# Weight loads ahead of a waiting load on SyncE's queue, in a fused sparse-attention and mixture-of-experts kernel

## Chip, cores and metric

The kernel runs on one core of a Trainium2 chip. The metric is the device time of one execution in microseconds (us); lower is better. A profiled execution gives a trace. Its span runs from the first to the last instruction, and the execution's own time is a little longer than its span.

## What is computed

First a block-sparse softmax attention over 4 batches, 8 heads, 768 positions and 64 channels, all in float32. Each block of 32 queries sees its own and the two neighbouring key blocks, the first and the last block, and three blocks that an index table names; the first and the last query block see all keys. The result, reordered to 3072 tokens of 512 channels, goes into a soft mixture of 8 experts with 4 slots each:

```python
attn = softmax(where(mask, q @ k.T / 8, -1e9)) @ v
x = attn.transpose(0, 2, 1, 3).reshape(3072, 512)
logits = x @ phi                                   # 512 x 32
slot_input = softmax_over_tokens(logits).T @ x     # 32 slots
h = relu(slot_input[e] @ w1[e])                    # 512 -> 1024, per expert
slot_out[e] = h @ w2[e]                            # 1024 -> 512
out = softmax_over_slots(logits) @ slot_out
```

The slots need the softmax over all tokens, so the experts cannot start before the attention has ended. The expert weights w1 and w2 are 33.5 MB together, in 64 tiles of 128 partitions by 1024 floats (512 KB each).

## The kernel before

The attention is a list of 52 items: per batch 11 pairs of query blocks (`plan_pair`) and two dense halves (`plan_dense`) for the first and the last block. An item is a chain over the engines. GpSimd (POOL) and ScalarE (ACT) stage the key blocks (`kst`); TensorE (PE) makes the scores (`s`, L652; `sd`, L849); VectorE (DVE) takes row maxima (L669, L867); ACT takes exponentials (L674, L880); DVE turns them (`ptt`, L681; `ptd`, L884); PE multiplies with the values (`av`, `avd`, L746); DVE normalizes the result to `x` (L739 to L741). Transposes of `x` (`mxt`, L940), the logits (`ml`, L975) and the running slot sums (`ms`, L1025) follow per group of four query tiles. At the end of the attention four groups of logits are normalized (`cm`, `lst`, L1083 to L1100), split into two halves each (`c`, L1107 on DVE and L1113 on POOL) and transposed (`pc`, L1126) for the last matmul.

The order of this part is not the order of the source. A `Plan` object collects tasks with their dependencies and buffers; `plan` simulates the engines with fixed task costs and takes, among the tasks that can start soonest, the one with the smallest `turn`; `turn` is the task's key in items plus `BEHIND[kind]`, one number for each of 82 kinds of task. `run` then issues the tasks in that order inside a manual schedule, which keeps the issued order on PE, DVE, ACT and POOL, and inside a second one, which keeps it on SyncE (SP). All large DMAs are issued by SP, one after the other: an SP instruction that waits holds up all those behind it.

The planner also paces DMAs. It counts PE instructions in packets of 256 (a matmul of the program is four of them) and ties a paced DMA to a PE instruction at `MARK` = 56 instructions into a packet (`gate`); after `ROOM` = 0.55 MB behind one gate, or 1.4 us after it (`LATEST`), the next DMA has to take the next gate. `run` writes the tie as a wait on that PE instruction (`wait`).

The weights are loaded in the order in which the experts use them. Tiles 0 to 10 have places of their own (`wpre`) and come in during the attention. Tiles 11 to 25 go into places that the last batch leaves: the keys of the batch before (`ktile`, shown as `kw`), the values buffer `v0`, the buffer `ptd`, and then the keys' other buffer (`kw` again, tiles 23 to 25, the group with `n0 == 12`, from item 12 of the last batch on). These are tasks of the plan. The late tiles 26 to 43 are issued after `plan.run()` by `load_late`, one for each entry of `LORD`:

```python
LORD = [0, 1, 2, 3, 4, 5, -1, -2, -3, -4, 6, 7, 8, 9, -5, -6, 10, 11]
load_late(..., late + LATE * (2 * min(k, SLOW) + max(k - SLOW, 0)))
```

Entries from 0 on are places that the staging buffers of the attention leave (`lwb`, tile names w26 to w31, then w36 to w39) or places of `ptt`; negative entries are the six places in the values buffer `v1`, which the last matmuls of the attention read. Each of these loads waits on the last gate that the plan puts ahead of its due time. They are issued outside the second schedule, so on SP the framework's own scheduler decides their order. Tiles 44 to 63 take the places of tiles that the first expert layer has used (`done_w`, `next_w`).

The experts' two layers are `ffn1` (`pf`, L1370) and `ffn2` (`pso`, L1378), in two halves of the output columns. When the first half's slots are there, its outputs are made (`po`, L1474), copied (`ob`, L1476 and L1478) and stored between the experts of the second half; the second half's outputs follow at the end. At most eight SP DMAs are under way, since each waits for the landing of the one eight places before it.

Of the kernel before, what the change touches and what calls it, by code (L numbers as in the profile page):

```python
# [21 lines left out]
P = 128  # L22
# [20 lines left out]

LR, RATE = 64, 0.22
ROOM, AFTER, LATEST, NEXT = 0.55e6, 0.1, 1.4, 5.5
MARK, LATE, SLOW = 56, 1.1, 5

CS = 2
CW = DM // CS
# [1 line left out]
WP = 2048 // PW  # L51
# [11 lines left out]
E_ = mybir.EngineType  # L63
MAN = {E_.PE, E_.DVE, E_.Activation, E_.Pool}

BEHIND = {0: -25.15, 1: -115, 2: -27.9, 3: -173.9, 4: 29, 5: 50.5, 6: 234.65, 7: -47.25, 8: -98, 9: -36.5, 10: -8.25,
# [8 lines left out]
SOON = 0.03  # L75
LAG = {"DVE": 0.17, "ACT": 0.18, "POOL": 0.17, "SP": 0.0, "NONE": 0.0}
SP_COST = 0.55
# [32 lines left out]
class Plan:  # L110
# [30 lines left out]
    def plan(self, turn, best=1e9):  # L141
        T = self.tasks
        at = {e: 0.8 for e in ("PE", "DVE", "ACT", "POOL", "SP", "NONE")}
        mode, count, okay, room = "T", FIRST, 0.0, ROOM
# [13 lines left out]
        while avail:  # L158
            cand = []
            for t in avail:  # L160
                r, ok, k = ready[t], True, {}
                for p in need[t]:
                    i = (nxt[p] + k.get(p, 0)) % pools[p]
                    k[p] = k.get(p, 0) + 1
                    if held[p][i] or (p in queue and queue[p][qat[p]] != t):
                        ok = False
                        break
                    if slot[p][i] > r:
                        r = slot[p][i]
                if not ok:  # L170
                    continue
                if pace[t]:
                    r = max(r, at["SP"], gate + AFTER)
                    if r < gate + NEXT and (room <= 0 or r > gate + LATEST):
                        r = gate + NEXT
                st, en, e, d = 1e9, 1e9, None, None
                for o, c in opts[t]:
                    if o == "PE":
                        c = PE_TASKS[c]
                        s = at[o] if c[2] == mode else at[o] + TURN[mode]  # L180
                        if r > s:
                            s = r
                        z = s + c[0]
                    else:
                        s = at[o] if at[o] > r else r
                        z = s + c
                    if s < st or (s == st and z < en):
                        st, en, e, d = s, z, o, c
                cand.append((st, turn[t], en, t, e, d))
# [5 lines left out]
            if pace[t]:  # L195
                if st >= gate + NEXT:
                    gate, room, gid = st, ROOM, None
# [108 lines left out]
def attn_moe_kernel(ctx, tc, qT, kT, vtab, sampled, phi, w1, w2, out):  # L306
# [847 lines left out]
    N = len(items)  # L1154
# [24 lines left out]

    m, n = NPRE, first[B - 1]  # L1180
    t_last = state.t_acc
    for tag, pool, n0, n1 in (("ktile", "k", 1, 3), ("v0", "v", 3, 6), ("ptd", "ptd", 5, 7), ("ktile", "k", 12, 13)):
        go = lambda j: [qks[min(N - 1, n + n0 + (n1 - n0) * j // KW[tag])]]
        a_w = add(lambda t, tag=tag: new_wk(tag), ("NONE", 0.0), go(0), N + m, acq=[(pool, [t_last])])
        for j in range(KW[tag]):
            parts = [(slice(r, r + LR), slice(0, WP)) for r in range(0, P, LR)]
            if n0 == 12:
                parts = [(slice(0, P), slice(0, WP))]
            for i, (r, c) in enumerate(parts):
                add(lambda t, m=m, tag=tag, j=j, r=r, c=c: load_wk(m, tag, j, r, c), ("SP", SP_COST), go(j) + [a_w],  # L1190
                    N + m + j + i / 4, byte=4 * WP * P // len(parts), pace=2 if n0 == 12 else 1)
        m += KW[tag]


# [92 lines left out]
    ms = tc.manual_schedule(engines=MAN)  # L1287
    ms.__enter__()
    plan.fill = max(qks.items())[1], lambda n: warm(None, n)
    with tc.manual_schedule(engines={E_.SP}):  # L1290
        plan.run()
    warm(None, 1)
    ssum = fin.tot
    att.close()
# [31 lines left out]
    def load_late(pool, j, due):  # L1326

        m = len(wpool)
        i = load_w(m, pool) if j is None else load_wk(m - j, pool.tag, j)
        plan.wait(i, [plan.names[k] for k, b in enumerate(plan.bounds) if b[2] + AFTER <= due][-1])  # L1330
        wpool.append(pool)
# [21 lines left out]
    for k, n in enumerate(LORD):  # L1353
        if n < 0:
            load_late(vw, -1 - n, late + LATE * (2 * min(k, SLOW) + max(k - SLOW, 0)))
        else:
            load_late(lw[n], None, late + LATE * (2 * min(k, SLOW) + max(k - SLOW, 0)))

    def done_w(n):

# [206 lines left out]
```

## Time and profile before

| | us |
|---|---|
| median of 3 runs (308.28, 311.31, 311.51) | 311.31 |
| the profiled execution's own time | 310.53 |
| its span | 308.8 |
| PE busy | 279.3 |
| DVE busy | 217.1 |
| POOL busy | 178.9 |
| ACT busy | 173.8 |

A row of the timeline gives the start, the length, the engine, line, operation and tiles and a count; in brackets stands the idle time before it and what ended it. `SPq` is SyncE's queue; a row of DMAs there is the time of issuing, not of the transfer. Attention and slot sums run to about 248.7 us, the experts from 248.75 us (the first `pf`) to 291.86 us (the last `pso`), the last outputs to 300.45 us (the last copy `ob`), and the stores to the end.

### The profile page before, as it was taken

Reading aid. Unit: us, or ns where it says so; the run is one execution under the profiler, and the core shown is the slowest. Engines: PE = TensorE matmul, PEld = TensorE weight load, DVE = VectorE, ACT = ScalarE, POOL = GpSimd, SP = SyncE. Lnnn points to the kernel's source line nnn. Section 1 sums busy time; section 2 is a strip of 40 time slices with the busy share of each in tenths; the row PEclk is TensorE's granted clock in tenths of the full one; section 3 lists DMA queues with packets and bytes.
Section 4 is the critical chain, followed back from the end, with each engine's and each line's share of the span. In section 5 each row is a group of like instructions: output and inputs, shape, how many; then the busy total and the mean of one; then the engine's idle time right before and its main releaser. Section 6 shows DMA issues by size and latency. Waiting matters only on the chain.

```text
span 308.8 us, 17460 instructions
## 1 busy us (share of the span) xinstructions
PE 279.3 (90%) x7177; PEld 195.4 (63%) x7177; DVE 217.1 (70%) x500; ACT 173.8 (56%) x525; POOL 178.9 (58%) x491
## 2 busy tenths in 40 slices
PE   8598999999999999999999999979998999988670
PEld 7168777567777686686776768658676734534260
DVE  7779978778899789989997699877794250112160
ACT  7965976754685876477777637747431411004250
POOL 6668699956559998745899757369654140000000
PEclk9979999999999999999999999999999999999976
DMA  7924555373254547345454666557644899999998
GB/s 242 242 52 129 145 142 132 98 190 90 89 143 139 145 133 192 88 108 138 136 142 130 172 160 155 150 140 188 171 140 143 290 413 409 408 408 407 393 330 288
DMA packets 27825, 60.27 MB, mean 195 GB/s; under 512 B 3553, under 2 KB 16994, under 8 KB 27746
## 3 DMA queue, kind: packets, MB, share of 16 engines
q1 hardware_dynamic: 27600, 59.03, 62.2%
q8 instruction: 56, 0.92, 1.3%
q14 instruction: 23, 0.19, 0.2%
q10 hardware_dynamic: 146, 0.13, 0.1%
HBM read 52.86 MB, written 6.29 MB: 192 GB/s over the span
## 4 chain that ended last, share of the span: by engine, by line
PE 65%; DMA 18%; DVE 7%; issue 3%; SPq 2%; ACT 1%; ACTq 0%
PE av L746 32%; DMA w<-in_w_dram 13%; PE s L652 13%; PE avd L746 7%; PE mxt L940 4%; DMA kw<-in_w_dram 3%; PE sd L849 3%; PE po L1474 2%; DMA ktile<-in_kT_dram 2%; PE ml L975 2%; PE ms L1025 2%; DVE ptt L681 2%; DVE x L741 1%; DVE nm L669 1%; SPq L333 1%
## 5 line engine op out<-in xcount | busy, mean ns | idle before, releaser
L593 POOL COPY vrs<-v 128x260 f32 x264 | 95.4, 405 | 27.7 <-PE av L746 17.2
L674 ACT ACTIVATE p<-s,nm 128x256 f32<-128x256 f32 x176 | 72.7, 475 | 13.5 <-DVE nm L669 11.5
L746 PE MATMUL av<-v,ptt 64*64 64x130 f32 (+2 forms) x1728 | 76.2, 288 | 0.5 <-issue 0.5
L746 PEld LDWEIGHTS av<-v,ptt 64*64 64x64 f32 (+2 forms) x1728 | 50.7, 133 | 25.6 <-issue 19.0
L681 DVE STREAM_TRANSPOSE ptt<-p 128x512 f32<-128x512 f32 x88 | 56.3, 682 | 3.8 <-ACT p L674 3.7
L669 DVE TENSOR_REDUCE nm<-s 128x2 f32<-128x512 f32 x88 | 55.2, 679 | 2.2 <-PE s L652 2.0
L652 PE MATMUL s<-kst,q 64*32 64x256 f32 x1408 | 51.1, 380 | 2.6 <-ACT pd L880 1.8
L746 PE MATMUL av<-vrs,ptt 64*32 64x130 f32 x2112 | 46.9, 278 | 2.7 <-issue 2.6
L575 ACT ACTIVATE kst<-ktile 128x128 f32 x186 | 41.4, 303 | 10.1 <-PE s L652 8.9
L569 POOL COPY kst<-ktile 128x384 f32<-128x384 f32 x88 | 42.4, 507 | 6.2 <-PE s L652 6.2
L652 PEld LDWEIGHTS s<-kst,q 64*32 64x32 f32 x1408 | 31.2, 106 | 13.0 <-POOL vrs L593 3.1
L746 PEld LDWEIGHTS av<-vrs,ptt 64*32 64x32 f32 x2112 | 36.4, 106 | 4.7 <-issue 4.3
L467 ACT COPY xT<-mxt 128x512 f32<-128x512 f32 (+1 forms) x22 | 12.4, 564 | 23.2 <-PE mxt L940 22.8
L746 PE MATMUL avd<-v,ptd 64*64 64x130 f32 x768 | 23.7, 271 | 1.8 <-DVE ptd L884 1.2
L746 PEld LDWEIGHTS avd<-v,ptd 64*64 64x64 f32 x768 | 21.9, 132 | 4.0 <-PE s L652 2.1
L613 POOL TENSOR_SCALAR q<-q 128x256 f32<-128x256 f32 x21 | 8.4, 404 | 22.2 <-DMA q<-in_qT_dram 22.2
L577 POOL COPY kst<-ktile 128x128 f32 x78 | 20.0, 295 | 0.0
L880 ACT ACTIVATE pd<-sd,nb 128x384 f32<-128x384 f32 x32 | 16.8, 577 | 5.4 <-DVE nb L875 4.7
L611 ACT ACTIVATE q<-q 128x256 f32<-128x256 f32 x27 | 11.1, 418 | 13.7 <-DMA q<-in_qT_dram 13.1
L739 DVE TENSOR_SCALAR rs<-av 128x8 f32<-128x8 f32 (+1 forms) x27 | 4.1, 153 | 20.3 <-PE av L746 20.2
L940 PEld LDWEIGHTS mxt<-ident,x 128*128 128x128 f32 x96 | 10.2, 141 | 12.6 <-PE sd L849 2.9
L940 PE MATMUL mxt<-ident,x 128*128 128x128 f32 x96 | 15.9, 286 | 2.4 <-DVE x L728 0.9
(122 smaller groups left out, 312.0 us busy)
## 6 DMA issues: line engine op xcount, KB each, us to landing
w<-in_w_dram SPq DMA_DIRECT2D x23, 512.0 KB, 10.2
v<-in_w_dram SPq DMA_DIRECT2D x12, 512.0 KB, 10.2
q<-in_qT_dram SPq DMA_DIRECT2D x47, 128.0 KB, 2.8
w<-in_w_dram SPq DMA_DIRECT2D x22, 256.0 KB, 4.1
out_dram<-ob SPq DMA_DIRECT2D x22, 256.0 KB, 3.9
ktile<-in_kT_dram SPq DMA_DIRECT2D x24, 192.0 KB, 3.4
v<-in_vtab_dram SPq DMA_DIRECT2D x16, 211.2 KB, 3.9
v<-in_vtab_dram SPq DMA_DIRECT2D x16, 195.0 KB, 3.5
```

The source lines that it names most:

```text
L467: ACT.copy(out=out, in_=in_)
L569: POOL.tensor_copy(out=st[:, :, w:w + 96], in_=kv[:, :, (i - 1) * BLK:(i + 2) * BLK])
L575: ACT.activation(out=st[:, :, o:o + BLK], in_=src, func=AF.Copy, scale=1.0)
L577: POOL.tensor_copy(out=st[:, :, o:o + BLK], in_=src)
L593: POOL.tensor_copy(out=st[:, :, j:j + 1, :], in_=vf[:, :, ds(t.vals[j], 1), :])
L652: PE.matmul(u.s[r][32 * p:32 * p + 32, j, :], lhsT=u.q[s_, p, j, :], rhs=kd[j][0][s_, p, :], start=True, stop=True)
L669: DVE.tensor_reduce(out=u.nm[r], in_=u.s[r], axis=AX.X, op=ALU.max, negate=True)
L674: ACT.activation(out=u.p[r][:, j, :], in_=u.s[r][:, j, :], func=AF.Exp, bias=u.nm[r][:, j:j + 1], scale=1.0)
L681: DVE.transpose(out=T.pt[r][:, :, 2 * w:2 * w + 2, :].rearrange("p k j q -> p j k q"), in_=u.p[r].rearrange("p j (k q) -> p j k q", k=8))
L746: PE.matmul(av[:, r * 2 * D1:(r + 1) * 2 * D1].rearrange("p (a d) -> p a d", a=2), lhsT=lhsT, rhs=rhs, start=start, stop=stop)
L880: ACT.activation(out=u.p[r][k], in_=u.s[r][k], func=AF.Exp, bias=u.nb[r], scale=1.0)
L940: PE.transpose(T.px[:, c, :], T.x[:, c * P:(c + 1) * P], ident)
```

## The change

Five edits; everything else is as before.

1. The schedule that keeps SP's issued order is left only after the loop over `LORD`, so the late loads stand in the order in which the source issues them.
2. The group of tiles 23 to 25 may start at item 11 of the last batch and not at item 12 (the `12` in its tuple and in the two comparisons is `11`).
3. A task of that group (`pace == 2`) is no longer sent to the next gate when the 0.55 MB are used up.
4. `LATE`, the step of the late loads' due times, is 1.0 us and not 1.1 us.
5. All 82 numbers of `BEHIND` are new.

```diff
-MARK, LATE, SLOW = 56, 1.1, 5
+MARK, LATE, SLOW = 56, 1.0, 5
...
-BEHIND = {0: -25.15, 1: -115, 2: -27.9, 3: -173.9, 4: 29, 5: 50.5, 6: 234.65, 7: -47.25, 8: -98, 9: -36.5, 10: -8.25,
+BEHIND = {0: 14.2, 1: -87.35, 2: 8.05, 3: -200, 4: -26.55, 5: 41.95, 6: 286.05, 7: -87.5, 8: 25.85, 9: -26.95, 10:
...
                 if pace[t]:
                     r = max(r, at["SP"], gate + AFTER)
-                    if r < gate + NEXT and (room <= 0 or r > gate + LATEST):
+                    if r < gate + NEXT and (room <= 0 and pace[t] == 1 or r > gate + LATEST):
                         r = gate + NEXT
...
-    for tag, pool, n0, n1 in (("ktile", "k", 1, 3), ("v0", "v", 3, 6), ("ptd", "ptd", 5, 7), ("ktile", "k", 12, 13)):
+    for tag, pool, n0, n1 in (("ktile", "k", 1, 3), ("v0", "v", 3, 6), ("ptd", "ptd", 5, 7), ("ktile", "k", 11, 12)):
...
-            if n0 == 12:
+            if n0 == 11:
                 parts = [(slice(0, P), slice(0, WP))]
...
-                    N + m + j + i / 4, byte=4 * WP * P // len(parts), pace=2 if n0 == 12 else 1)
+                    N + m + j + i / 4, byte=4 * WP * P // len(parts), pace=2 if n0 == 11 else 1)
...
-    with tc.manual_schedule(engines={E_.SP}):
-        plan.run()
+    ls = tc.manual_schedule(engines={E_.SP})
+    ls.__enter__()
+    plan.run()
...
             load_late(lw[n], None, late + LATE * (2 * min(k, SLOW) + max(k - SLOW, 0)))
+    ls.__exit__(None, None, None)
```

How this moves instructions. On SP, at the end of the attention, with the semaphores that each DMA waits for (`PE_49` is a wait on a PE instruction, `DMAHW` the wait for the DMA eight places before), the program had:

```order
L333 DMA ptd_67<-in_w1_dram 64x1024 [waits DMAHW3_49,PE_49]
L333 DMA kw_6562<-in_w1_dram 128x1024 [waits DMAHW4_49,PE_49,Activation_49]
L333 DMA kw_6562<-in_w1_dram 128x1024 [waits DMAHW5_49]
L333 DMA kw_6562<-in_w1_dram 128x1024 [waits DMAHW6_49,PE_49]
L333 DMA v1_69<-in_w2_dram 128x1024 [waits DMAHW7_49,PE_49,Pool_49]
L333 DMA w26_7026<-in_w1_dram 128x1024 [waits DMAHW0_49]
L333 DMA w27_7028<-in_w1_dram 128x1024 [waits DMAHW1_49]
L333 DMA w28_7030<-in_w1_dram 128x1024 [waits DMAHW2_49]
L333 DMA w29_7032<-in_w1_dram 128x1024 [waits DMAHW3_49]
L333 DMA w30_7034<-in_w1_dram 128x1024 [waits DMAHW4_49]
L333 DMA w31_7036<-in_w1_dram 128x1024 [waits DMAHW5_49]
```

and has now:

```order
L333 DMA ptd_67<-in_w1_dram 64x1024 [waits DMAHW3_49,PE_49]
L333 DMA kw_6517<-in_w1_dram 128x1024 [waits DMAHW4_49,Activation_49,Pool_49]
L333 DMA kw_6517<-in_w1_dram 128x1024 [waits DMAHW5_49]
L333 DMA kw_6517<-in_w1_dram 128x1024 [waits DMAHW6_49,PE_49]
L333 DMA w26_7025<-in_w1_dram 128x1024 [waits DMAHW7_49]
L333 DMA w27_7027<-in_w1_dram 128x1024 [waits DMAHW0_49]
L333 DMA w28_7029<-in_w1_dram 128x1024 [waits DMAHW1_49]
L333 DMA w29_7031<-in_w1_dram 128x1024 [waits DMAHW2_49,PE_49]
L333 DMA w30_7033<-in_w1_dram 128x1024 [waits DMAHW3_49]
L333 DMA w31_7035<-in_w1_dram 128x1024 [waits DMAHW4_49,PE_49,Pool_49]
L333 DMA v1_69<-in_w2_dram 128x1024 [waits DMAHW5_49,Pool_49]
```

The load into `v1` stood ahead of six loads and stands behind them. The values of the waits, counted in PE's matmuls of the program: before, the first `kw` waits for number 3211, the third for 3264 and the load into `v1` for 3342; now the third `kw` waits for 3211, w29 for 3277 and w31 for 3342. Number 3264 is the last matmul of the second last pair's `av`, 3277 the third and 3342 the 68th of the 84 of the last pair's. Behind these rows the two programs have the same loads in the same order.

On DVE the last item before was (`c` is the split of a group of logits, the `x` ahead of it is what PE's next transposes `mxt` read):

```order
L1100 TENSOR_TENSOR lst<-lst,cm 128x128
L681 STREAM_TRANSPOSE ptt<-p 128x2x8x32 x4
L739 TENSOR_SCALAR rs<-av 128x8
L740 RECIPROCAL rs<-rs 128x8
L741 TENSOR_TENSOR x<-av,rs 128x512
L1107 TENSOR_SCALAR c_6751<-lst 128x4x32 x2
```

and is now:

```order
L1100 TENSOR_TENSOR lst<-lst,cm 128x128
L681 STREAM_TRANSPOSE ptt<-p 128x2x8x32 x4
L1107 TENSOR_SCALAR c_6727<-lst 128x4x32 x2
L739 TENSOR_SCALAR rs<-av 128x8
L740 RECIPROCAL rs<-rs 128x8
L741 TENSOR_TENSOR x<-av,rs 128x512
```

One pair of `c` moved ahead of `x`. At the starts of the second, third and fourth batch DVE's order differs too, and in a like manner; at the last of them (the dense scores `sd`, with two transposes `ptt` of the pair before) it was:

```order
L681 STREAM_TRANSPOSE ptt<-p 128x2x8x32
L867 TENSOR_REDUCE nm<-sd 128x1 x2
L875 TENSOR_TENSOR nb_5207<-nm 128x1
L469 COPY d<-md 128x128
L867 TENSOR_REDUCE nm<-sd 128x1 x2
L875 TENSOR_TENSOR nb_5273<-nm 128x1
L884 STREAM_TRANSPOSE ptd<-pd 128x12x32 x2
L681 STREAM_TRANSPOSE ptt<-p 128x2x8x32
```

and is now:

```order
L681 STREAM_TRANSPOSE ptt<-p 128x2x8x32 x2
L469 COPY d<-md 128x128
L867 TENSOR_REDUCE nm<-sd 128x1 x2
L875 TENSOR_TENSOR nb_5266<-nm 128x1
L867 TENSOR_REDUCE nm<-sd 128x1 x2
L875 TENSOR_TENSOR nb_5274<-nm 128x1
L884 STREAM_TRANSPOSE ptd<-pd 128x12x32 x2
```

The second `ptt` and the copy `d` moved ahead of the maxima over `sd`. PE's own order differs in three places: twice a transpose `mxt` trades places with its neighbour `lt`, and once one moves a pair later. The DMAs ahead of the rows shown keep their order on SP and the PE instructions that they wait for.

16 rows, old and new, of the table BEHIND are left out of this document.

## The prediction

> **What bounds the kernel now.** I read the page's slices first, then the stretches of the last 90 us, then SyncE's queue, the chain, and PE's waits. The slices (40 of 7.72 us) show two different kernels:
>
> ```profile
> PE   8598999999999999999999999979998999988670
> DMA  7924555373254547345454666557644899999998
> GB/s 242 242 52 129 145 142 132 98 190 90 89 143 139 145 133 192 88 108 138 136 142 130 172 160 155 150 140 188 171 140 143 290 413 409 408 408 407 393 330 288
> ```
>
> Up to about 240 us PE is full and the DMA engines are half idle; from slice 32 on (247 us) the DMA engines are full at some 408 GB/s and PE has holes. So the last quarter is bound by how early the weight stream starts. The stretches around its start, with the columns PE, PEld, DVE, ACT, POOL, clock, DMA share and GB/s:
>
> ```profile
> 219.00:226.50 7.50, 7.46 (x224) 5.52 (x217) 5.30 (x16) 3.00 (x12) 4.50 (x13) 1.00 0.49 142
> 226.50:232.00 5.50, 4.85 (x111) 4.00 (x110) 5.33 (x17) 0.30 (x2) 2.79 (x8) 1.00 0.65 197
> 232.00:236.50 4.50, 4.50 (x163) 3.52 (x166) 1.55 (x4) 0.46 (x1) 2.70 (x7) 1.00 0.32 117
> 236.50:238.50 2.00, 1.14 (x26) 0.80 (x15) 1.48 (x10) 0.24 (x1) 0.00 (x0) 1.00 0.46 129
> 250.00:291.20 41.20, 36.06 (x418) 16.13 (x410) 8.08 (x24) 6.43 (x13) 3.57 (x6) 1.00 1.03 407
> 291.20:308.80 17.60, 7.46 (x38) 5.69 (x38) 5.52 (x11) 4.80 (x10) 0.00 (x0) 0.77 0.94 317
> ```
>
> Between 219 and 238.5 us the DMA engines move 117 to 197 GB/s; afterwards 407 until the last weight has landed, and in the last 17.6 us, stores of short rows, they are still 94% busy. Why the stream starts late is on SyncE's queue:
>
> ```profile
> 213.12 9.01 SPq L333 DMA_DIRECT2D ptd<-in_w_dram  x6
> 226.47 2.92 SPq L333 DMA_DIRECT2D kw<-in_w_dram  x3
> 236.48 0.33 SPq L333 DMA_DIRECT2D v<-in_w_dram  x1
> 236.86 5.16 SPq L333 DMA_DIRECT2D w<-in_w_dram  x6
> 242.06 5.89 SPq L333 DMA_DIRECT2D v<-in_w_dram  x3
> SPq L333 <- PE av L746: 28.6, 11, 7.0
> ```
>
> After the third `kw` (issued by 229.4 us) the queue stands still for 7.0 us, its longest wait, until the last `av` has read the values; the load into `v1` that waits stands ahead of six loads (w26 to w31) that wait for nothing. From there on the chain is the stream itself, each link being the landing that lets the DMA eight places later go:
>
> ```profile
> 240.11 9.79 DMA w<-in_w_dram
> 249.92 10.20 DMA w<-in_w_dram
> 260.18 10.16 DMA w<-in_w_dram
> 270.35 10.58 DMA kw<-in_w_dram
> 281.00 10.19 DMA w<-in_w_dram
> 291.22 0.64 PE pso L1378 x8
> ```
>
> Eight tiles take 10.2 us, so one tile of 512 KB costs 1.28 us, and the last expert matmuls start when the last tile lands.
>
> **The change, part by part.** *Late loads in the source's order (edit 1), with LATE (edit 4).* As the order of SyncE's queue shows, w26 to w28 now follow the third `kw` with no wait on an engine, w29 and w30 follow at matmul 3277 and w31 at 3342. Before, the first `kw` waited for 3211 and went at 226.47 us, and the `v1` load waited for 3342 and went at 236.48 us; these rows date the gates. Number 3277 is the third matmul of the last `av`, which starts at 231.8 us (row below). So the third `kw` goes at 226.5, w26 to w28 by about 228.5, w29 and w30 at about 232, w31 at 236.5 and the six `v1` loads behind it. Five tiles (w26 to w30) are moved ahead of 236.5 us, when the engines have room: the room from 226.5 to 236.5 us is ten us, and three `kw` and five tiles take 8 x 1.28 = 10.2 us. At 236.5 us the rest of the stream is five tiles shorter: 5 x 1.28 = **6.4 us**. The bounds of this term: at most 1.4 us more, if w30 is still under way when w31 goes, so that the start-up hole of 236.5 to 238.5 us (129 of 407 GB/s, 1.4 us lost) closes; at least 3 x 1.28 = 3.8 us, if w29 and w30 get no room ahead of w31.
>
> *The keys' old place one item sooner, and its pace (edits 2 and 3).* The first two `kw` lose their PE gate and follow the last `ptd`, which is issued by 222.1 us; the third, whose issue ended at 229.4 us, goes some 2 us sooner. What they wait for on ACT and POOL is staging of keys for the last scores, and these scores run at 221.6 us (first row below). That makes the room that the five tiles need (0.49 busy from 219 to 226.5 us); by itself it is worth nothing, since these tiles are used well after 250 us. Without it about two tiles less would fit: that is the lower bound just named.
>
> *Does the rest follow?* Behind w31 the queue's waits are on the eighth load before and on gates already passed, save w42, which waits for the matmul `msum`, and the loads from w44 on, which wait for the first expert layer:
>
> ```profile
> 221.57 1.12 PE L652 MATMUL s<-kst,q 64*32 64x256 f32 x31
> 247.24 0.36 PE L1224 MATMUL msum<-ssum,selw 128*128 128x1 f32 x2
> 248.75 4.92 PE L1370 MATMUL pf<-w,sT 128*32 128x512 f32 x42 [0.38 <-ACT sT L467]
> ```
>
> With 11 tiles (14 us) let go after 236.5 us the engines have work until after 250 us; `msum` runs at 247.2 us and the first layer starts at 248.75. It takes some 0.45 us for a tile (4.92 us for 11 tiles), so it frees places faster than the 1.28 us in which they are filled. No hole. On the other side PE must be able to finish sooner:
>
> ```profile
> 270.36 3.63 PE L1378 MATMUL pso<-w,hT 128*32 128x256 f32 x64
> 274.60 0.64 PE L1378 MATMUL pso<-w,hT 128*32 128x256 f32 x8
> 275.88 0.64 PE L1378 MATMUL pso<-w,hT 128*32 128x256 f32 x8 [0.64 <-DMA w<-in_w_dram]
> PE pso L1378 <- DMA w<-in_w_dram: 2.5, 4, 0.6
> PE pso L1378 <- DMA v<-in_w_dram: 1.6, 3, 0.6
> PE pso L1378 <- DMA kw<-in_w_dram: 1.1, 2, 0.6
> ```
>
> PE never waits for a tile before 274.6 us; after it, it waits 2.5 + 1.6 + 1.1 = 5.2 us up to 291.86 us. Taking just these out, the experts would end at 286.7. But eight such matmuls cost 0.64 us alone and 3.63 / 8 = 0.45 in a row, and 14 groups save another 2.6: 284.0 at best. With the stream 6.4 us ahead they end at 285.4, between the two: PE stops being idle just where the stream stops being late. So I keep 6.4, with 5.2 as a bound. The stores are behind the weights on the same saturated engines, so the end moves with the stream.
>
> *The new BEHIND table (edit 5).* DMAs ahead of `kw` keep order and gates, PE's order hardly changes, so it acts through DVE. The last item:
>
> ```profile
> 227.57 2.48 DVE L681 STREAM_TRANSPOSE ptt<-p 128x512 f32<-128x512 f32 x4
> 230.38 0.69 DVE L741 TENSOR_TENSOR x<-av,rs 128x512 f32<-128x512 f32 x1
> 230.98 2.56 DVE L1107 TENSOR_SCALAR c<-lst 128x128 int32<-128x128 int32 x8
> 231.21 0.63 PE L940 MATMUL mxt<-ident,x 128*128 128x128 f32 x4 [0.65 <-DVE c L1107]
> 231.84 4.58 PE av L746 x128
> ```
>
> PE already waits 0.65 us there, for `x`, with filler matmuls before it and the last `av` behind it. Two `c` now stand ahead of `x`: 2 x 2.56 / 8 = 0.64 us later, with nothing to hide it. **Loss 0.6 us**, and the gate 3342 is as much later. At the three batch starts one `ptt` (2.48 / 4 = 0.62) and one `d` copy (of the size of a `c`, 0.32) move ahead of the dense maxima, 0.9 us each. PE has the pair's `av` and the next scores to run meanwhile, so I cost it at nothing; without that cover it is 2.7 us lost, and a `ptt` that is ready sooner could give back as much.
>
> *PE's instructions.* They come by DMA too, and a load ahead of them can hold them up:
>
> ```profile
> q8 instruction: 56, 0.92, 1.3%
> 197.99 1.90 SPq L427 DMA_DIRECT2D q<-in_qT_dram  x2
> 199.94 1.11 SPq L333 DMA_DIRECT2D v<-in_w_dram  x2
> 204.15 0.43 PE L746 MATMUL av<-vrs,ptt 64*32 64x130 f32 x12 [1.63 <-issue]
> ```
>
> These are 56 packets of 16 KB, 256 instructions each. After 0.75 MB of loads PE stood 1.63 us with nothing else to wait for, the largest such hole. Now 2.1 MB (third `kw`, w26 to w28) go out just before the packet boundary near 232 us, and a packet lasts 128 matmuls there, 4.6 us. Of those 2.1 MB (4 x 1.28 = 5.1 us from about 228.5) some 1.6 us remain at 232, as much as 0.75 MB (1.8 us) did in the other place; but three `kw`, 1.5 MB, left no such hole. **Loss 0.3 us**, between 0 and 1.6.
>
> [...]
>
> The sum: 308.8 - 6.4 + 0.6 + 0.3 = **303.3 us** of span. The profiled execution took 310.53, 1.7 more than its span, so **305.0 us**. The median of the runs shown is 0.8 above that execution, their lowest 2.3 below; I make no correction.
>
> **The rivals.** *PE becomes the bound (B).* The experts end at 286.7 plus the 0.9 us lost before: gain 5.2 - 0.9 = 4.3, **306.2 us**. For it: the 0.64 us groups; against it: 0.45 us in a row. *Fewer tiles get ahead (C).* If only w26 to w28 find room, 3.8 - 0.9 = 2.9: **307.6 us**. For it: the gates of w29 and w31; against it: the share of 0.32 from 232 to 236.5 us. *The packet waits in line (D).* If PE's instructions wait behind all that is queued, six tiles (third `kw`, w26 to w30) are 7.7 us against the 4.6 that a packet lasts: a hole of 3.1 us, gain 6.4 - 0.6 - 3.1 = 2.7: **307.8 us**, hardly measurable. For it: the hole after 0.75 MB; against it: the three `kw` before. *DVE holds PE up (E), slower.* If at each of the three batch starts the dense scores wait for a full row of transposes, 2.48 us, the attention ends 3 x 2.48 + 0.6 = 8.1 us later, and every gate and the first layer with it: 308.8 + 8.1 - 6.4 = 310.5, that is **312.2 us**. It decides from 6.4 us of new stalls on. Against it: what moves is one transpose, not four, and PE's longest sum of waits for DVE before is at another place and small:
>
> ```profile
> PE avd L746 <- DVE ptd L884: 1.2, 2, 0.8
> ```
>
> **How the numbers follow.** Forecast (A) 0.57, B 0.18, C 0.08, D 0.11, E 0.06. The range: from 302.3 (6.4 + 1.4 without the small losses, and half a us of luck in the order) up to 308.8, past D and short of E, which leaves out some 0.15. A measurement here tells about 1% from no change, 3.1 us (the three runs lie 3.2 apart). Faster by more: all of A and B, half of C and a quarter of D, less a little for the scatter: 0.79. Within 1%: the rest of C and D and a part of E: 0.16. Slower: 0.05.
>
> **What would show it.** In SyncE's rows five `w` loads between 226 and 234 us and no wait of 7 us; over 300 GB/s from 228 to 236 us; the first `pf` at 249 to 250 us; the last `pso` at 285 to 287; little wait of `pso` for DMA; `x` of the last item 0.6 us later than its `av`. I am wrong if the first `pf` comes after 252 us, if holes by issue grow by over 2 us between 228 and 240, or if the last tile lands after 288.

## The result and the profile after

The changed kernel took 301.0 us (median of four runs, 299.22 to 301.57), the kernel before on the same chip 309.86 (four runs): a ratio of 0.9736, 95% interval 0.9686 to 0.9787. On a second chip it was 301.93 us against 310.45, 0.9806 (0.9738 to 0.9874). I had predicted 305.0 against 310.53, a ratio of 0.982: faster, but on the first chip too little, where the median lies 1.3 us below my range. On the second chip the ratio that I had forecast lies inside the interval, and the median 0.4 us below the range. The ratios leave out disturbed executions, which the medians include; the profiled ones of e2_loads and e10_loads were disturbed and are not shown, and those of the kernel before, e5_due and e13_q are longer than their medians (by 0.7, 2.4 and 3.5 us), so no conclusion rests on their whole time.

The profiled run of the changed kernel took 301.57 us, its span 299.8 (before 308.8). The slices of its page, 7.5 us each:

```profile
PE   7689999999999999999999999899997899999870
DMA  7924555373355556435445575656799699999998
GB/s 237 249 66 140 137 155 142 108 180 93 91 135 144 151 142 163 113 90 159 120 134 167 135 178 168 166 138 168 183 276 316 213 371 409 407 408 408 383 321 278
```

The DMA engines are now busy from slice 29 on (217 us), slice 31 excepted, and not from 32 on. In stretches (columns as in the prediction):

```profile
217.00:224.50 7.50, 7.46 (x224) 5.64 (x207) 6.96 (x20) 3.01 (x11) 4.70 (x14) 1.00 0.92 269
224.50:230.00 5.50, 4.50 (x102) 3.60 (x102) 3.90 (x13) 0.58 (x1) 4.89 (x13) 1.00 0.96 329
230.00:234.50 4.50, 2.67 (x84) 1.82 (x84) 0.42 (x4) 0.00 (x0) 0.00 (x0) 1.00 0.67 210
248.00:281.00 33.00, 33.00 (x406) 16.57 (x402) 7.29 (x20) 6.43 (x13) 3.45 (x6) 1.00 1.03 407
281.00:299.80 18.80, 7.96 (x50) 5.71 (x38) 5.53 (x11) 4.81 (x10) 0.00 (x0) 0.78 0.94 314
```

Where 117 to 197 GB/s were moved, 210 to 329 are. In the experts both PE (33.00 of 33.00 us) and the DMA engines (1.03) are full. SyncE's queue from the `kw` on:

```profile
217.49 4.55 SPq L333 DMA_DIRECT2D kw<-in_w_dram  x3
222.09 11.83 SPq L333 DMA_DIRECT2D w<-in_w_dram  x6
234.01 2.94 SPq L333 DMA_DIRECT2D v<-in_w_dram  x4
237.05 3.65 SPq L333 DMA_DIRECT2D w<-in_w_dram  x4
```

The six `w` follow the three `kw` at once, and the wait of 7.0 us is gone. On PE, the last scores-and-values stretch and the experts:

```profile
226.95 0.63 PE L940 MATMUL mxt<-ident,x 128*128 128x128 f32 x4 [0.56 <-DVE c L1107]
232.82 0.31 PE L746 MATMUL av<-v,ptt 64*32 64x130 f32 x4 [1.28 <-issue]
245.89 4.91 PE L1372 MATMUL pf<-w,sT 128*32 128x512 f32 x42 [0.38 <-ACT sT L467]
282.11 0.64 PE L1380 MATMUL pso<-w,hT 128*32 128x256 f32 x8 [0.63 <-DMA w<-in_w_dram]
```

So the time came from two places. From the first `pf` to the end of the last `pso` it was 248.75 to 291.86, 43.11 us, and is 245.89 to 282.75, 36.86: 6.25 us less. And the first `pf` itself comes 2.86 us sooner, where I had it 0.9 later. Behind the last `pso` 16.94 us have become 17.05.

### The profile page after: what moved, and what is told of

The parts are those of the page before. It is cut to its first block, busy times and chain, and to the rows that moved or that the text cites. A ratio compares the mean times of both kernels' runs of the same rounds, so it can differ in the third digit from the quotient of the medians.

```text
span 299.8 us, 17458 instructions
## 1 busy us (share of the span) xinstructions
PE 275.7 (92%) x7177; PEld 194.9 (65%) x7177; DVE 217.0 (72%) x500; ACT 174.5 (58%) x528; POOL 178.2 (59%) x488
## 4 chain that ended last, share of the span: by engine, by line
PE 70%; DMA 12%; DVE 6%; issue 3%; POOL 2%; POOLq 2%; SPq 1%; ACT 1%; ACTq 0%; DVEq 0%
PE av L746 30%; PE s L652 11%; PE avd L746 6%; PE pf L1372 5%; DMA q<-in_qT_dram 5%; PE mxt L940 4%; DMA w<-in_w_dram 4%; PE sd L849 3%; PE pso L1380 2%; DMA v<-in_vtab_dram 2%; PE ms L1025 2%; PE ml L975 2%; PE po L1476 2%; POOLq L455 1%; DVE ptt L681 1%
## 5 line engine op out<-in xcount | busy, mean ns | idle before, releaser
L746 PE MATMUL av<-v,ptt 64*64 64x130 f32 (+2 forms) x1728 | 75.3, 285 | 1.4 <-issue 1.3
L746 PEld LDWEIGHTS av<-v,ptt 64*64 64x64 f32 (+2 forms) x1728 | 49.9, 131 | 26.9 <-issue 19.6
L746 PE MATMUL av<-vrs,ptt 64*32 64x130 f32 x2112 | 46.1, 275 | 1.3 <-issue 1.2
L746 PEld LDWEIGHTS av<-vrs,ptt 64*32 64x32 f32 x2112 | 35.7, 105 | 3.1 <-issue 2.0
L613 POOL TENSOR_SCALAR q<-q 128x256 f32<-128x256 f32 x18 | 7.2, 405 | 21.0 <-DMA q<-in_qT_dram 20.9
L611 ACT ACTIVATE q<-q 128x256 f32<-128x256 f32 x30 | 12.3, 418 | 12.4 <-DMA q<-in_qT_dram 11.7
L849 PE MATMUL sd<-ktile,q 64*32 64x384 f32 x256 | 16.6, 510 | 1.1 <-ACT p L674 0.6
```

The costliest lines, as they stand in the source:

```text
L746: PE.matmul(av[:, r * 2 * D1:(r + 1) * 2 * D1].rearrange("p (a d) -> p a d", a=2), lhsT=lhsT, rhs=rhs, start=start, stop=stop)
L849: PE.matmul(u.s[r][k][32 * p:32 * p + 32, :], lhsT=T.dq.q[s_, p, j, :], rhs=kt[s_, p, 384 * k:384 * (k + 1)], start=True, stop=True)
```

## Experiments

"Before" in this table is the kernel before on the same chip.

| run | what it is | median | before | ratio (95%) |
|---|---|---|---|---|
| e1_table | new table alone | 307.28 | 308.83 | 0.995 (0.9903 to 0.9997) |
| e2_loads | edits 1 to 4, old table | 302.61 | 308.83 | 0.9849 (0.9794 to 0.9904) |
| e10_loads | the same again | 305.23 | 310.45 | 0.986 (0.9752 to 0.9968) |
| e3_order | edit 1 alone | 308.27 | 308.83 | 0.9988 (0.9941 to 1.0035) |
| e4_keys | edits 2 and 3 alone | 309.11 | 308.83 | 1.0016 (0.997 to 1.0061) |
| e5_due | edit 1, earlier due times | 306.93 | 310.5 | 0.9902 (0.9856 to 0.9947) |
| e6_gate | changed kernel, one wait back | 307.69 | 310.5 | 0.9928 (0.9887 to 0.9968) |
| e7_hold | before, two loads held | 311.52 | 310.5 | 1.0082 (1.0034 to 1.0131) |
| e8_spread | changed kernel, w28 later | 302.45 | 310.5 | 0.9769 (0.9718 to 0.982) |
| e12_spread | the same again | 302.34 | 310.45 | 0.9821 (0.9745 to 0.9897) |
| e11_c | that, and `c` behind `x` | 302.5 | 310.45 | 0.9814 (0.9711 to 0.9916) |
| e9_after | changed kernel again | 301.93 | 310.45 | 0.9806 (0.9738 to 0.9874) |
| e13_q | before, one ScalarE task moved | 307.87 | 310.47 | 0.9934 (0.9891 to 0.9977) |
| e14_lq | edits 1 to 4, the same task moved | 302.91 | 310.47 | 0.9772 (0.9708 to 0.9836) |

### The edits one by one: e1_table, e2_loads, e3_order, e4_keys

Each takes some of the edits of the diff and leaves the rest: e1_table edit 5, e2_loads edits 1 to 4, e3_order edit 1, e4_keys edits 2 and 3.

> The kernel before with the new BEHIND table alone (edit 5); its loads keep their order and gates. Theory S (the loads' part is what the recorded sum said, 6.2 us of the experts' stretch; the 2.9 us by which the first pf came sooner are scatter of PE's instruction holes from run to run): no gain, 0 to 0.6 us slower, since the pair c stands ahead of x here too. Theory T (the table brought the 2.9 us, of which 4.7 had been gained by 218 us): 3 to 5 us faster, with the first pf 3 to 5 us sooner than 248.75 us and the experts' stretch unchanged at 43.1 us.

> The changed kernel with the old BEHIND table (edits 1 to 4 alone). Theory S: within 0.6 us of the changed kernel, that is about 9 us faster than before. Theory T: 4 to 6 us faster than before and 3 to 5 slower than the changed kernel. Both: the experts' stretch from the first pf to the end of the last pso of 36.9 us falls from 43.1, and a hole by issue of 1 to 1.3 us in the last av.

> The kernel before with edit 1 alone (SyncE keeps the source's order of the late loads; keys at item 12, LATE 1.1, old table). By its gates two tiles, w26 and w27 (at matmul 3277), get ahead of matmul 3342, and the v1 load no longer stands ahead of the six. If each tile ahead is worth its 1.28 us, as the recorded sum has it: 2.6 us faster. If what counts is the blocked queue as such and not the number of tiles ahead: as much as all edits on the loads, about 6 us.

> The kernel before with edits 2 and 3 alone (keys' old place from item 11, not sent to the next gate). No tile more gets ahead of the waiting v1 load, so by the recorded sum it is worth nothing: within 0.5 us of before. If sooner loads into the keys' place are worth something by themselves: 2 us or more.

The loads give 1.5%, and the table alone gives half a per cent, where I had costed it as a loss. e1_table fits neither of its theories: its first `pf` comes at 245.38 us, 3.4 us sooner than before, as theory T has it, but its experts take 44.27 us and not 43.11, and the time falls by 1.5 us. e10_loads, e2_loads again on the chip of e9_after, was expected 1.5 to 2.5 us above the changed kernel: 0.986 beside 0.9806 is some 1.7 us, with intervals that overlap. The surprise is the pair e3_order and e4_keys: neither edit 1 nor edits 2 and 3 move the time by themselves. In e3_order two tiles (w26, w27) do go ahead of the wait for matmul 3342. Of the kernel before, and then of e3_order, rows of SyncE's waits:

```profile
SPq L333 <- PE msum L1224: 4.1, 1, 4.1
```

```profile
SPq L333 <- PE av L746: 28.2, 13, 4.1
SPq L333 <- PE msum L1224: 6.6, 1, 6.6
```

What the loads no longer wait at the `av` (7.0 us, now 4.1 at most) they wait at a second place: the fourth load into `v1` waits for `msum`, matmul 3416, and holds up all behind it. In both programs it is the tenth of these loads (six `w` and four `v1`), and in both the tenth goes at about 247 us. Edit 1 alone only starts the queue for this wait sooner.

In the changed kernel the wait for `msum` is seven loads later, at w42. What takes it from the fourth `v1` load are edits 2 and 3: the due times of the late loads count from the plan's last paced load, and with the keys one item sooner that load, and so all due times, are 5.5 us earlier. In e4_keys, with the old `LATE`, that load goes at 242 us, ahead of `msum`, and no load waits for it. The shorter step of edit 4 makes the last due times up to 2.2 us earlier still; what it does to the place of the wait is not shown.

### Which part of edit 2 counts: e5_due, e6_gate

e5_due is e3_order with the due times moved and the keys left where they were; e6_gate is the changed kernel with the wait for `msum` put back to the fourth load into `v1`.

```diff
-MARK, LATE, SLOW = 56, 1.1, 5
+MARK, LATE, SLOW = 56, 1.0, 5
...
-    late = max(t.start for t in plan.tasks if t.eng == "SP") + 1.0
+    late = max(t.start for t in plan.tasks if t.eng == "SP") - 4.5
...
```

```diff
+        if m == 35:
+            plan.wait(i, plan.names[len(plan.bounds) - 1])
```

> The kernel before with edit 1 and with the late loads' due times 5.5 us earlier (as edits 2 and 4 make them), but the keys' place filled at its old time and the old table. On SyncE w26 to w28 then follow the third kw freely, w29 and w30 wait for matmul 3277, w31 for 3342, and the wait for msum (matmul 3416) moves from the fourth load into v1 to the sixth, seven loads later. Theory G (gates): edit 1 alone was worth nothing because the loads that it let go only came sooner to the wait for msum (4.1 us before, 6.6 us with edit 1 alone); with both waits out of the way five tiles gain 5 x 1.28 = 6.4 us even with the keys at their old time: 302.5 to 304 us beside about 308.8 of before. Theory R (room, the lower bound of my prediction): without the keys one item sooner only three tiles find room, 3.8 us: 305 us. Theory K: it is the keys' earlier place itself that gives the time: 308 to 309 us.

> The changed kernel with one wait moved: the fourth load into v1 waits for msum (matmul 3416) again, as it did before, and not w42 seven loads later. Theory G: nine loads (w26 to w31, three of v1) have gone by then; the last four of them go at about 234.5 us and have landed at about 240, and msum runs at 244.4 us: the engines stand some 4.5 to 6 us and the gain shrinks by as much: 305.5 to 307.5 us. Theory O (the order of the six loads carries the gain, the rest is only room): 301 us, as the changed kernel.

e6_gate lost most of the gain: 0.9928, 307.69 us, beside 0.9736 and 0.9806 of the changed kernel. Its rows of SyncE, and its wait:

```profile
224.97 11.01 SPq L333 DMA_DIRECT2D w<-in_w_dram  x6
236.08 11.05 SPq L333 DMA_DIRECT2D v<-in_w_dram  x4
SPq L333 <- PE msum L1224: 8.5, 1, 8.5
```

All five tiles stand ahead of gate 3342 in this kernel, and little is gained by it, since the stream then stops for 8.5 us: from the first `pf` to the last `pso` it takes 41.19 us, beside 43.11 before and 36.86 in the changed kernel. So the gain needs both waits out of the way. That is shown from both sides: e6_gate has the wait for `msum` alone, and e4_keys, no faster than before, has the one at the `av` (9.5 us) and none for `msum`.

e5_due came out near the number of theory R, 0.9902, some 3 us faster, but not for its reason. The stream was on time: `pso` waits 0.3 us for DMA in all, and the stretch from the first `pf` to the last `pso` is 36.53 us, as short as in the changed kernel, with the keys at their old time. The time went on PE, in the last `av`. One execution was profiled, so how long the hole is in the others is not shown. Rows of SyncE, of PE, and of the DMA queues from 229.9 to 236.0 us and from 236.0 to 237.2:

```profile
224.16 2.92 SPq L333 DMA_DIRECT2D kw<-in_w_dram  x3
227.13 12.91 SPq L333 DMA_DIRECT2D w<-in_w_dram  x6
238.51 0.44 PE L746 MATMUL av<-v,ptt 64*32 64x130 f32 x4 [4.84 <-issue]
254.01 4.50 PE L1372 MATMUL pf<-w,sT 128*32 128x512 f32 x40 [0.38 <-ACT sT L467]
```

```profile
DMA packets 514, 1.88 MB, mean 308 GB/s; under 512 B 56, under 2 KB 56, under 8 KB 513
q1 hardware_dynamic: 513, 1.87, 97.5%
...
q1 hardware_dynamic: 124, 0.45, 95.9%
q8 instruction: 1, 0.02, 5.6%
```

PE stands 4.84 us from 233.7 us on, at the four matmuls of the last `av` where the changed kernel stands 1.28. In the 6.1 us up to 236.0 the loads move 1.87 MB and no packet of PE's instructions (q8) moves; one moves by 237.2, and PE goes on at 238.51. It looks as my rival D has it, in another kernel. So filling the keys one item sooner does make room, but in this profile what comes late without it is PE's instruction packet and not the tiles.

### PE's instruction packets: e7_hold, e8_spread, e12_spread, e9_after

e7_hold moves two loads of the kernel before behind the next packet boundary; e8_spread sends w28 of the changed kernel to the later gate. e9_after and e12_spread are the changed kernel and e8_spread again, on one chip.

```diff
+        late = [t for t in order if t.n in (1127, 1128)]
+        order = [t for t in order if t not in late]
+        at = [t.n for t in order].index(1129)
+        order[at:at] = late
+        for t in late:
+            self.gates[t.n] = 44
```

```diff
-            load_late(lw[n], None, late + LATE * (2 * min(k, SLOW) + max(k - SLOW, 0)))
+            load_late(lw[n], None, late + LATE * (2 * min(k, SLOW) + max(k - SLOW, 0) + 2 * (k == 2)))
```

> The kernel before with one thing changed: two loads of 256 KB into v0 go behind the next q load, and so wait for matmul 2886 and not for 2822. They then start behind the boundary of PE's instruction packet near 199 us instead of just ahead of it. Theory F: the hole of 1.1 to 1.6 us in the av at matmul 5669 of the trace (204 us) is PE's instruction packet that waits behind these loads; it falls below 0.3 us and the time by some 1.0 to 1.6 us, to about 307.5 beside 308.8. Rival: the hole is something of that place in the program (it stays over 1 us and the time stays at 308.8). Third: the hole moves to the next boundary, time the same.

> The changed kernel with w28 sent behind matmul 3277, as w29 and w30 are, so that one tile of 512 KB less lies ahead of the packet boundary at 227.7 us. Theory F: the delay of that packet falls from 2.7 us by up to 1.28, the hole of 1.28 us in the last av falls to 0.0 to 0.6, the first pf comes about 1 us sooner and, since PE is full in the experts, the end too: 299.8 to 300.5 us beside 301.0. Rival: the stream is what bounds still, and a tile sent later costs up to 1.28 us: 301.5 to 302.3 us.

> The changed kernel with w28 behind matmul 3277, again, on the same chip as the changed kernel. Theory F: no hole over 0.3 us in the last av, first pf about 1.2 us sooner than in the changed kernel, time 0.5 to 1.2 us below it. Rival: the time is that of the changed kernel or above, since the packet waits at the next boundary in its place (3.7 us of delay there in the first profile) or the tile is missed later.

> The changed kernel again, on the same chip as the three below, to be compared with them. 0.973 of before (0.969 to 0.979 in its first runs): some 301 us. The hole by issue in the last av, 1.28 us, should be there again if PE's instruction packet waits behind the same loads each time.

In e7_hold the hole of 1.63 us at matmul 5669 shrank to 0.53 (theory F had it below 0.3), and others opened. Rows of PE:

```profile
211.90 0.76 PE L752 MATMUL av<-vrs,ptt 64*32 64x130 f32 x35 [1.20 <-issue]
236.99 0.31 PE L752 MATMUL av<-v,ptt 64*32 64x130 f32 x4 [1.83 <-issue]
```

The time rose by 0.8% (0.3 to 1.3). The third forecast, that the hole moves, is nearest, though it had the time unchanged: the loads taken off one boundary came onto others.

In e8_spread the hole of the last `av` is gone, and the first `pf` comes 1.2 us sooner than in the first profile of the changed kernel. But in e9_after the unchanged program has it no longer either: 0.18 us instead of 1.28.

```profile
232.41 0.31 PE L746 MATMUL av<-v,ptt 64*32 64x130 f32 x4 [0.18 <-issue]
```

And on one chip e12_spread took 302.34 us and e9_after 301.93, and its first `pf` came 1.4 us later (246.86 against 245.49 us). So the later w28 gains nothing that can be measured, and the rival holds.

For that one packet fourteen profiles give a row each. The trace has every DMA packet's start. In the profiles of before and after the twelve holes by issue of over 0.2 us all stand 193 or 194 past a multiple of 256 in the count of PE's records. The delay is counted from 24 records ahead of the multiple of 256 before the hole's place (an estimate: of the 112 packets of before and after, the starts lie from 19 records ahead of such a point to 175 behind it), and the KB are what the loads moved meanwhile.

```text
kernel      KB moved   delay us   hole us
e4_keys         0        0.28       under 0.3
e8_spread     196        0.66       under 0.3
e12_spread    216        0.81       under 0.3
e1_table      320        0.89       under 0.3
before        432        1.42       under 0.3
e11_c         512        1.46       under 0.3
e9_after      656        1.54       0.18
e6_gate       760        1.74       0.46
e3_order      636        2.13       0.73
e13_q         476        2.29       1.00
after        1012        2.74       1.28
e14_lq       1040        2.95       1.55
e7_hold       696        3.21       1.83
e5_due       1904        6.19       4.84
```

The hole is the delay less 1.3 to 1.5 us wherever there is one: that much of this packet's delay shows in no hole. The delay grows with the KB moved, loosely: 0.28 us with none, 1.46 with 512, 2.95 with 1040 and 6.19 with 1904, but 3.21 with 696 in e7_hold.

### The pair of `c` on DVE: e11_c

e8_spread, with the first pair of `c` behind `x` again, by one dependency in the plan; PE's transposes `mxt` also stand ahead of some filler matmuls here that they follow in e8_spread.

```diff
-        self.prepare()
+        self.tasks[1160].after.append(self.tasks[941]); self.prepare()
```

> The kernel with w28 behind matmul 3277 (as in the run of the label e12_spread), and the first two c behind x on DVE again, as before the change. If the pair holds up x by 0.45 to 0.6 us and PE with it, PE's wait at that mxt (0.56 to 0.79 us with the pair ahead) falls to 0.2 or less and the time falls by 0.4 to 0.6 us below e12_spread; if PE's fillers hide it, no change. Times this near can't be told by the medians alone; the wait and the first pf decide.

PE's wait at that `mxt` fell from 0.62 and 0.79 us (e9_after, e12_spread) to 0.26, and its releaser is `x` again:

```profile
227.43 0.63 PE L940 MATMUL mxt<-ident,x 128*128 128x128 f32 x4 [0.26 <-DVE x L741]
```

By this wait the pair costs 0.4 to 0.5 us at its place; I had 0.6. But PE's wait there differs as much between profiles with one order of the two (0.65 us before and 0.88 in e1_table, both with the pair behind). The stretch from matmul 6300 to 6450 of the trace, around that `mxt`, is steadier: 6.48 to 6.57 us in six profiles with the pair behind `x`, 6.95 to 7.18 in seven with it ahead, so 0.4 to 0.7 us; in e11_c, counted alike, it is 6.80 beside 7.17 and 7.18 of e8_spread and e12_spread.

The pair does not come with the new table. DVE in e4_keys (edits 2 and 3, old table) and in e1_table (new table alone):

```profile
227.41 0.68 DVE L1107 TENSOR_SCALAR c<-lst 128x128 int32<-128x128 int32 x2
228.44 0.69 DVE L741 TENSOR_TENSOR x<-av,rs 128x512 f32<-128x512 f32 x1
```

```profile
227.45 0.69 DVE L741 TENSOR_TENSOR x<-av,rs 128x512 f32<-128x512 f32 x1
228.05 2.15 DVE L1107 TENSOR_SCALAR c<-lst 128x128 int32<-128x128 int32 x7
```

With edits 2 and 3 the planner puts the pair ahead of `x`; with the table alone it stays behind. The prediction and the expectation for e1_table have this wrong.

The whole kernel did not gain in e11_c: 302.5 us beside 302.34, and `pso` waits 1.0 us for DMA (1.3 in e12_spread). No version was shown to be faster than the changed kernel.

### What in the new table gives time: e13_q, e14_lq

I cut the attention at fixed matmuls of the trace and compared the profiles. Up to matmul 6300 (221 to 226 us), ahead of nearly all that edits 1 to 4 touch, before, e3_order, e4_keys, e5_due and e7_hold (old table) took 222.85 us on average from the first matmul, and the seven profiles with the new table 220.75. Most of it is one stretch: from matmul 4500 to 4800, near 163 us, the old table takes 9.56 to 10.78 us and the new one 8.44 to 9.03. ScalarE there, in the kernel before and in the changed one:

```profile
161.37 0.42 ACT L611 ACTIVATE q<-q 128x256 f32<-128x256 f32 x1 [1.10 <-DMA q<-in_qT_dram]
161.69 0.46 ACT L674 ACTIVATE p<-s,nm 128x256 f32<-128x256 f32 x1
162.29 0.71 ACT L575 ACTIVATE kst<-ktile 128x128 f32 x3
162.91 0.94 ACT L674 ACTIVATE p<-s,nm 128x256 f32<-128x256 f32 x2
163.75 0.70 ACT L575 ACTIVATE kst<-ktile 128x128 f32 x3
164.35 0.46 ACT L674 ACTIVATE p<-s,nm 128x256 f32<-128x256 f32 x1
164.70 0.70 ACT L575 ACTIVATE kst<-ktile 128x128 f32 x3
```

```profile
160.61 0.42 ACT L611 ACTIVATE q<-q 128x256 f32<-128x256 f32 x1
160.93 0.45 ACT L674 ACTIVATE p<-s,nm 128x256 f32<-128x256 f32 x1
161.29 1.30 ACT L575 ACTIVATE kst<-ktile 128x128 f32 x6
```

Before, a scaling of `q` stands ahead of three stagings of keys and waits 1.10 us for its DMA. Everything behind it is late, and the last `kst` ends at 165.4 us, in the middle of the scores that read it. With the new table that scaling stands behind one staging and four exponentials and waits for nothing. e13_q gives the kernel before this one move; the order of all other engines stays. e14_lq does the same to edits 1 to 4.

```diff
-        self.prepare()
+        self.tasks[777].after.append(self.tasks[712]); self.tasks[758].after.append(self.tasks[777]); self.tasks[758].after.append(self.tasks[713]); self.prepare()
```

> The kernel before (old table) with one scaling of q on ScalarE, near 160 us, moved behind one staging of keys and four exponentials, as the new table has it; PE, DVE, POOL and SyncE keep their order. Theory Q (the scaling waits 1.0 to 1.3 us for its DMA and holds up the key staging behind it, and PE's scores with it): the stretch of PE from matmul 4500 to 4800 falls from 9.6 to 10.8 us to 8.5 to 9.1, as with the new table, and the packet's delay there is shorter too or does not matter; the time falls by 1.0 to 1.6 us, to about 0.996 of before. Theory P (PE's instruction packet at 163 us is the cause, delayed 1.4 to 3.5 us by 367 to 807 KB of loads): the stretch stays over 9.5 us and the time where it is.

> Edits 1 to 4 with the old table and the same scaling moved. Theory Q: the stretch from 4500 to 4800 takes 8.5 to 9.1 us, and of the 1.7 to 3.3 us that edits 1 to 4 alone lay above the changed kernel some 1.0 to 1.6 go: about 0.981 of before, 303.5 us beside 309.5. The rest, the hole near matmul 5669, stays. Theory P: as the run of edits 1 to 4 alone, 0.985.

The stretch took 8.91 us in e13_q and 8.83 in e14_lq. The scores of the kernel before, and of e13_q:

```profile
163.51 2.70 PE L652 MATMUL s<-kst,q 64*32 64x256 f32 x60
```

```profile
164.39 1.93 PE L652 MATMUL s<-kst,q 64*32 64x256 f32 x60
```

The time fell to 0.9934 (0.9891 to 0.9977), 2.1 us, and edits 1 to 4 with this move, 0.9772, are as fast as the changed kernel on its two chips, within the intervals. Theory Q holds, and theory P does not. The packet at 163 us does come sooner with it (delayed 1.33 us in e13_q, 2.61 before). The hole near matmul 5669, which I expected to stay, is 0.75 us in e13_q and 0.26 in e14_lq. So one task on ScalarE does what the 82 numbers do, as far as the times can tell.

## Why the prediction was right in sign and too small

**The stream, 6.4 us: right.** Five tiles went ahead of gate 3342, and from the first `pf` to the last `pso` 6.25 us are saved. The end moved with the stream as assumed. PE is full just where the stream stops being late: `pso` waits 0.6 us for DMA and not 5.2. Rival B named the right mechanism, but with the 0.64 us of an eight that waits; in a row they cost less (16 in 1.07 us in the changed kernel), as I argued against it.

**What this term needs: incomplete.** I wrote of the keys one item sooner that "by itself it is worth nothing" and bounded the term at 3.8 us without them. For the room, e5_due gave a number near that bound, by a hole of PE and not by tiles that found no place. And I did not see that the earlier due times, which come with this edit, take the wait for `msum` from the fourth `v1` load to w42. I named that wait where it stands now, and not that the kernel before lost 4.1 us at it. With that wait in its old place e3_order, with two tiles ahead, gains 0.4 us and not the 2.6 of the same sum, and e6_gate, with all five, saves 1.9 us in the experts and not 6.25.

**The new table: the step that failed.** "DMAs ahead of `kw` keep order and gates, PE's order hardly changes, so it acts through DVE." What it gives comes through ScalarE, as far as the runs show. I had read the change of order on DVE and PE, and costed ScalarE's at nothing without naming it. There one move is worth some 1.5 us of a PE stretch (9.56 to 10.78 us against 8.83 and 8.91) and 2.1 us of time (0.7 to 3.4). I had nothing in its place, so this alone takes the forecast from 305.0 to 302.9. That is a gain of 7.6 us instead of 5.5. Measured are 8.2 us on the first chip and 6.0 on the second (301.0 / 0.9736 - 301.0, and likewise 301.93 and 0.9806): the sum with this term lies between the two, and without it below both.

**The hole at matmul 5669.** I quoted it (1.63 us by issue) as a price for the new loads, and did not ask whether the table would move it. In the changed kernel the packet there is delayed 0.39 us and not 2.32, and the hole is gone. Over all profiles the stretch from 5400 to 5700 is shorter by only 0.6 us, since an `mxt` waits longer for `x` there (0.43 and 0.51 us in the changed kernel's first profile, none there in that of before).

**The pair of `c`, 0.6 us:** the size is right, 0.4 to 0.7 at its place, but it belongs to edits 2 and 3 and not to the table, to which I put it down. So of the table's own part the sum held nothing at all. **The packet of the last `av`, 0.3 us, between 0 and 1.6:** 1.28 us in one profile and 0.18 in the other.

**What is left.** To matmul 6300 the changed kernel's first profile is 4.74 us ahead of the one of before. 1.5 us are the scaling's stretch and 1.3 the stretch of the hole at 5669. The 1.9 us that remain lie at the start (0.99) and between matmuls 1200 and 1500 (1.36), less what is given back elsewhere, and the old-table profiles differ from each other by as much at these two places (22.38 to 23.81 us, and 9.76 to 11.02). I put them down to scatter of the executions. e3_order supports it: its orders are those of before on all engines up to there, and it reaches matmul 6300 at 223.97 us and not at 225.62. Behind matmul 6300 the changed kernel gives back 1.9 us up to the first `pf`, 1.4 of them in the last `av` and 0.5 around the pair of `c`.

**The base.** The sum starts from one execution of 310.53 us, and I made "no correction". The measured ratio sets the changed kernel against some 309 us (301.0 / 0.9736). So about 1.4 us of the distance to 301.0 lie in the start and not in a mechanism.

## What to carry to other kernels

List all waits of an in-order queue, with what each holds up, before pricing the removal of the longest: the work let go arrives at the next wait (in e3_order the one for `msum` grew from 4.1 to 6.6 us). When an order changes, compare every engine that PE's inputs come through, and look first for an instruction that waits for a DMA with ready work behind it, since moving one such instruction took 2.1 us off in e13_q. Count how many bytes of loads lie ahead of PE's next instruction packet, because a gain in the stream can be lost there (a hole of 4.84 us in e5_due, with 1.87 MB of loads moved first).

## What the runs showed of the hardware

At the packet of the last `av` a delay up to 1.3 to 1.5 us shows in no hole; what is beyond shows as a hole "by issue" of that length, up to 4.84 us with 1.9 MB moved meanwhile. At matmul 5669 of the kernel before the difference is 0.7 (a delay of 2.32 us, a hole of 1.63). At both places, where there is a hole, PE goes on 2.3 to 2.9 us after the packet's start (230.48 and 232.82 us in the changed kernel, 201.42 and 204.15 before). Up to 432 KB of loads none of the five profiles has a hole of 0.3 us at the packet of the last `av`; from 476 KB on seven of nine have one of 0.46 to 4.84 us, and e11_c (512 KB) and e9_after (656 KB) have none of 0.3.

In e5_due 513 of the trace's packets, 1.87 MB of loads, move in the 6.1 us up to 236.0 us, and none of PE's instructions. Whether the loads went first at the DMA engines or PE asked late is not shown by any run here.
